# Uneven loads for uneven DMA engines: output weights and a few MLP rows split by numbers of partitions, in a single-token attention and MLP kernel

## The chip, the cores and the metric

The kernel runs on one core of a Trainium2 chip. A core has a matrix engine (TensorE, PE in the profile), a vector engine (VectorE, DVE), a scalar engine (ScalarE, ACT), GpSimd (POOL), a queue engine that issues transfers (SyncE, SP), and 16 DMA engines that move the bytes between the chip's main memory (HBM) and the core's on-chip memory. The on-chip memory has 128 partitions (rows); a tile such as `[128, 8, 512]` lies with its first index on the partitions.

The metric is the device time of one execution in microseconds. Before the change it is 194.83 us, the median of two runs (194.55 and 195.11). The profile shown is of one execution, with a span of 193.2 us.

## What is computed

One token passes a layer norm, and then two branches: attention over a cached window of 4096 positions with 32 heads, and a small MLP whose result gates it. Cut to what matters (all inputs are bf16):

```python
D, H, Dh, W, F = 512, 32, 128, 4096, 1376
xn = layernorm(x)                                    # x: [1, 1, 512]
# branch A
q = (xn @ wq)                                        # wq: [512, 4096] -> 32 heads of 128
k, v = k_cache[:, :, -W:], v_cache[:, :, -W:]        # [32 heads, 4096, 128] each
p = softmax(q @ k.T * Dh ** -0.5)                    # per head
s = (p @ v).reshape(1, 4096) @ wo                    # wo: [4096, 512]
# branch B: z = layernorm(xn); the first part's shifts leave only zeros for one token
x1 = xn + zeros @ w2
m = x1 + gelu(layernorm(x1) @ w3) @ w4               # w3: [512, 1376], w4: [1376, 512]
out = x + s * silu(m)
```

The keys and values of the window are 32 MiB each, the weights some 11 MB more. All of it is read once.

## The kernel before

The heads are worked off in eight groups of four (`G = 4`). The loop runs ten times: in step `s` the keys of group `s` are loaded and scored, and the values of group `h = s - 2` are loaded and weighted. There are three buffers for keys and two for values. A load of keys or values of one group is 4 MB, on 128 partitions of 32 KB.

All large loads go through one helper, and so through one issuing queue, in program order:

```python
def load(dst, src):
    return tc.keep_in_program_order(nc.sync.dma_start(out=dst, in_=src))
```

The start of the program (two small loads of x go through ScalarE's queue instead):

```python
nc.scalar.dma_start(out=x_bf[:], ...)                # 1 KB
nc.scalar.dma_start(out=x_row[0:P:32, :], ...)       # 1 KB, 4 partitions
load(w2_sb[:], ...)                                  # 512 KB
load(w3_sb[:], ...)                                  # 1376 KB
load(w4_sb[:, 0:10, :], ...)                         # 1280 KB
load(w4_sb[0:96, 10, :], B_w4[10 * P:F, :])          # the last 96 rows of w4, 1 KB each
load(wq_sb[:]..., A_wq.rearrange("(a b c) n -> b a (c n)", a=2, c=KC))   # 4 MB
...                                                  # then, in the loop, keys and values
```

The semaphores that report a load's completion are given out by the framework; the kernel's text names none.

The output weights `wo` have 32 row blocks of 128 rows, one for each head. They are used in four pieces:

```python
blocks = [(0, 16), (16, 8), (24, 8)]   # first head, number of heads
few_block = 2
few_h = 24
FEW = 8 * 8 * NE                       # NE = 5: 320 rows
h_part = few_h + FEW // P              # 26
r_part = FEW % P                       # 64

def load_wo(i):                        # heads 0-15, heads 16-23: n KB per partition
    h0, n = blocks[i]
    load(wo_blk[i], A_wo[h0 * P:(h0 + n) * P, :].rearrange("(p t) n -> p t n", p=P))

def load_few():                        # heads 24, 25 and half of 26: 2 x 20 partitions of 8 KB
    t = wo_blk[few_block]
    for c in range(2):
        r0 = few_h * P + c * FEW // 2
        load(t[32 * c:32 * c + 4 * NE],
             A_wo[r0:r0 + FEW // 2, :].rearrange("(b a t) n -> a b (t n)", b=4, a=NE))

def load_rows(h, n):                   # one row per partition for each head; half of head 26 first
    if h == h_part:
        load(wo_rows[r_part:P, 0, :], A_wo[h * P + r_part:(h + 1) * P, :])
        h, n = h + 1, n - 1
    load(wo_rows[:, h - h_part:h - h_part + n, :],
         A_wo[h * P:(h + n) * P, :].rearrange("(h p) n -> p h n", p=P))
```

A block that lies with several rows on one partition needs its attention output spread over the partitions in the same order: `ox_spread` (VectorE) and `ox_pick` (one matmul and two VectorE operations) do this with masks made at the start; for the 20-partition part `ox_few` adds a matmul with a selector `few` and a copy. `y_block` and `y_head` then add the products to the output row, as matmuls of 1x128.

The loop, cut to the loads and to the last two steps:

```python
for s in range(NG + LAG):              # NG = 8, LAG = 2
    h = s - LAG
    last = h == NG - 1
    kn = load_kv(k_pool, A_k_cache, s, ...) if s < NG else None
    ...
    if last:
        load_rows(h_part, 2)                               # rest of head 26, head 27
        v = load_kv(v_pool, A_v_cache, h, (0, 64, 112, CP))  # 2048, 1536 and 512 KB
        for r, n in ((H - G, 2), (H - 2, 1), (H - 1, 1)):  # heads 28-29, 30, 31
            load_rows(r, n)
    elif h >= 0:
        v = load_kv(v_pool, A_v_cache, h)
    if h == 3:
        load_wo(0)
    if h == 5:
        load_wo(1)
        load_few()
    ...
    elif s == NG:                                          # the seventh group of values
        ...; y_block(1); v_part(h, v); v_out(h)
        ox_spread(few_block); ...; ox_pick(few_block); ox_few(few_block)
    else:                                                  # the last group of values
        v_part(h, v, 0, cuts[1])
        y_block(few_block)
        for r in range(h_part, H - G):
            y_head(r)
        ...                                                # rest of the values
        v_out(h)
        for r in range(H - G, H):
            y_head(r)
# y = y_ps * g_row; out_row = y + x_row; store
```

Of the kernel before, what the change touches and what calls it, by code (L numbers as in the profile page):

```python
# [8 lines left out]
P = 128  # L9
BF16 = mybir.dt.bfloat16  # L10
FP32 = mybir.dt.float32
# [7 lines left out]
G = 4  # L19
LAG = 2  # L20
K_BUFS = 3
NE = 5
# [7 lines left out]
def kernel(  # L30
# [14 lines left out]
    nc = tc.nc  # L45

    Bb, Sq, D = A_x.shape
# [9 lines left out]
    KC = D // P  # L57
# [20 lines left out]
    def load(dst, src):  # L78
        return tc.keep_in_program_order(nc.sync.dma_start(out=dst, in_=src))
# [9 lines left out]
    load(w3_sb[:], B_w3.rearrange("(p c) n -> p c n", p=P))  # L89
    w4_sb = wts.tile([P, 11, D], BF16, name="w4_sb")  # L90
    load(w4_sb[:, 0:10, :], B_w4[0:10 * P, :].rearrange("(p c) n -> p c n", p=P))
    load(w4_sb[0:96, 10, :], B_w4[10 * P:F, :])
    wq_sb = wts.tile([P, KC, HD], BF16, name="wq_sb")

    load(wq_sb[:].rearrange("p c n -> p (c n)"), A_wq.rearrange("(a b c) n -> b a (c n)", a=2, c=KC))

    def load_kv(pool, cache, g, cuts=(0, CP)):
        t = pool.tile([P, CP, Dh], BF16, tag="kv", name="kv")
# [48 lines left out]
    def rows_add(ps, col, w, last):  # L147
        k = col.shape[0]
        for j in range(KC):
            nc.tensor.matmul(ps[32 * j:32 * j + 1, :], lhsT=col, rhs=w[0:k, j * P:(j + 1) * P],  # L150
                             start=False, stop=last, skip_group_check=True)
# [31 lines left out]
    nc.vector.tensor_copy(out=xn_bf[:], in_=xn_f[:])  # L183


    perm = wts.tile([P, P // 2, 2], BF16, name="perm")
    nc.vector.tensor_copy(out=perm[:], in_=ident_bf[:].rearrange("k (a b) -> k b a", a=2))
    xq_ps = ps_tr.tile([P, KC], FP32, tag="pt", name="xq_ps")
    nc.tensor.matmul(xq_ps[:], lhsT=perm[:].rearrange("k b a -> k (b a)"), rhs=xn_bf[:], start=True, stop=True)
    xq_bf = small.tile([P, KC], BF16, name="xq_bf")  # L190
# [67 lines left out]
        nc.scalar.copy(out=q_bc[:, i:i + 4, :], in_=qb_ps[:])  # L258
    make_masks(16)
    make_masks(8)  # L260

    few = const.tile([P, 2, 32], BF16, name="few")
    nc.vector.memset(few[:], 0.0)
    for c in range(2):
        nc.vector.tensor_copy(
            out=few[:, c, 0:4 * NE].rearrange("p (a b) -> p a b", b=4),
            in_=ident_bf[:, 4 * NE * c:4 * NE * (c + 1)].rearrange("p (b a) -> p a b", b=4))

# [107 lines left out]

    blocks = [(0, 16), (16, 8), (24, 8)]
    few_block = 2
    few_h = blocks[few_block][0]
    FEW = 8 * 8 * NE
    h_part = few_h + FEW // P

    r_part = FEW % P
    o_blk, wo_blk, ox_blk = {}, {}, {}

    def load_wo(i):
        h0, n = blocks[i]
        load(wo_blk[i], A_wo[h0 * P:(h0 + n) * P, :].rearrange("(p t) n -> p t n", p=P))

    def load_few():
        t = wo_blk[few_block]
        for c in range(2):  # L400
            r0 = few_h * P + c * FEW // 2
            load(t[32 * c:32 * c + 4 * NE],
                 A_wo[r0:r0 + FEW // 2, :].rearrange("(b a t) n -> a b (t n)", b=4, a=NE))

    def wo_row(h):
        return wo_rows[:, h - h_part, :]

    def load_rows(h, n):
        if h == h_part:
            load(wo_rows[r_part:P, 0, :], A_wo[h * P + r_part:(h + 1) * P, :])  # L410
            h, n = h + 1, n - 1
        load(wo_rows[:, h - h_part:h - h_part + n, :],
             A_wo[h * P:(h + n) * P, :].rearrange("(h p) n -> p h n", p=P))

# [25 lines left out]
    def v_out(g):  # L440
        h = G * g
        b = [i for i, (h0, _) in enumerate(blocks) if h >= h0][-1]
        if b not in o_blk:
            o_blk[b] = sm_pool.tile([P, blocks[b][1]], BF16, tag=f"o{b}", bufs=1, name="o")
            if b == few_block:
                nc.gpsimd.memset(o_blk[b][:], 0.0)
        c = h - blocks[b][0]
        if g >= NG - 2:
            nc.vector.tensor_tensor(out=o_blk[b][:, c:c + G], in0=st[g]["oT"][:], in1=st[g]["rden"][:],  # L449
                                    op=ALU.mult)  # L450
            return
        for k in range(G):
            nc.scalar.mul(o_blk[b][:, c + k:c + k + 1], st[g]["oT"][:, k:k + 1], st[g]["rden"][:, k:k + 1])  # L453


    def ox_spread(i):
        n = blocks[i][1]
        to, mt, mh = masks[n]
        spread = sm_pool.tile([P, n, n], BF16, tag=f"spread{n}", bufs=1, name="spread")
        nc.vector.tensor_tensor(out=spread[:], in0=o_blk[i][:].unsqueeze(2).to_broadcast([P, n, n]),  # L460
                                in1=mt[:].unsqueeze(1).to_broadcast([P, n, n]), op=ALU.mult)
        ox_blk[i] = spread
# [12 lines left out]
                                    op=ALU.add)  # L475
        ox_blk[i] = ox

    def ox_few(i):
        of_ps = ps_misc.tile([64, 8], FP32, tag="misc", name="of_ps")
        nc.tensor.matmul(of_ps[:], lhsT=few[:].rearrange("p a b -> p (a b)"), rhs=ox_blk[i][:],  # L480
                         start=True, stop=True)
        of = sm_pool.tile([64, 8], BF16, tag="of", bufs=1, name="of")
        nc.vector.tensor_copy(out=of[:], in_=of_ps[:])
        ox_blk[i] = of


    y_row = small.tile([1, D], FP32, name="y_row")

    yr = {}
# [9 lines left out]
            nc.scalar.copy(out=y_row[:], in_=yr[i][:])  # L499

    def y_block(i):
        for t in range(8):
            rows_add(y_ps, ox_blk[i][:, t:t + 1], wo_blk[i][:, t, :], False)

    def y_head(h):
        rows_add(y_ps, o_blk[few_block][:, h - few_h:h - few_h + 1], wo_row(h), h == H - 1)

    NG = H // G
    cuts = (0, 64, 112, CP)
# [4 lines left out]
    for s in range(NG + LAG):  # L514
        h = s - LAG
        last = h == NG - 1
        kn = load_kv(k_pool, A_k_cache, s, (0, 64, CP) if s == 0 else (0, CP)) if s < NG else None
        if s == LAG:
            wts_guard.__exit__(None, None, None)
            v_pool = ctx.enter_context(tc.tile_pool(name="v", bufs=V_BUFS))  # L520
            wo_blk[few_block] = v_pool.tile([64, 8, D], BF16, tag="wo_few", bufs=1, name="wo_few")
            nc.gpsimd.memset(wo_blk[few_block][:], 0.0)
            wo_rows = v_pool.tile([P, H - h_part, D], BF16, tag="wo_rows", bufs=1, name="wo_rows")
            nc.gpsimd.memset(wo_rows[0:r_part, 0, :], 0.0)
        if last:
            load_rows(h_part, 2)
            v = load_kv(v_pool, A_v_cache, h, cuts)
            for r, n in ((H - G, 2), (H - 2, 1), (H - 1, 1)):
                load_rows(r, n)
# [3 lines that stand above are left out]
            wo_24 = k_pool.tile([P, 32, D], BF16, tag="kv", name="wo_24")  # L533
            wo_blk[0], wo_blk[1] = wo_24[:, 0:16, :], wo_24[:, 16:24, :]
            load_wo(0)
        if h == 5:
            load_wo(1)
            load_few()

        if s < NG:  # L540
            nb = len(batches(s))

            def keys(b0, b1):
                for b in range(b0, b1):
                    k_turn(s, kn, b)
                    if b > 0:
                        k_scores(s, b - 1)

            k_open(s)
            k_vector(s, kn, 0)  # L550
            keys(0, 2)
            if s > 1:
                sm_den(s - 2)
                sm_rden(s - 2)
            if h - 1 in MOVED:
                v_add(h - 1)
                v_out(h - 1)
            keys(2, 4)
            k_vector(s, kn, 1)
            if s > 0:  # L560
                sm_turn(s - 1)
            if s == 6:
                ox_spread(0)
            keys(4, nb)
            k_scores(s, nb - 1)
            sm_own(s)
            if s > 0:
                sm_exp(s - 1)
            k_vector(s, kn, 2)
            if s == 6:  # L570
                ox_pick(0)
            k_vector(s, kn, 3)
            if h >= 0:
                v_part(h, v)
            sm_max(s)
            if s == 6:
                y_wide(0, 0, 16)
            if h >= 0 and h not in MOVED:
                v_out(h)
        elif s == NG:  # L580

            sm_den(NG - 2)
            sm_rden(NG - 2)
            sm_turn(NG - 1)
            ox_spread(1)
            sm_exp(NG - 1)
            ox_pick(1)
            y_block(1)
            rows_add(y_ps, one_f, y_row, False)
            v_part(h, v)  # L590
            v_out(h)
            ox_spread(few_block)
            sm_den(NG - 1)
            sm_rden(NG - 1)
            ox_pick(few_block)
            ox_few(few_block)
        else:
            v_part(h, v, 0, cuts[1])
            y_block(few_block)
            for r in range(h_part, H - G):  # L600
                y_head(r)
            for c0, c1 in zip(cuts[1:], cuts[2:]):
                v_part(h, v, c0, c1)
            v_out(h)
            for r in range(H - G, H):
                y_head(r)
# [36 lines left out]
```

## Time and profile before

| | |
|---|---|
| time, median of two runs | 194.83 us |
| span of the profiled execution | 193.2 us |
| read from main memory | 78.84 MB, 408 GB/s over the span |
| TensorE matmul busy | 132.6 us (69%) |
| VectorE busy | 143.8 us (74%) |
| ScalarE busy | 87.1 us (45%) |
| GpSimd busy | 6.4 us (3%) |
| shares of the chain that ended last | VectorE 50%, DMA 24%, TensorE 16% |

How to read the page. The span is cut into 40 equal slices; a digit is the busy share of an engine in a slice in tenths, 9 for 90% or more. The row named DMA is the mean busy share of the 16 DMA engines, and the row below it is what they moved. A queue's line gives its packets, its megabytes, and the time of its packets as a share of 16 engines times the span. The chain that ended last is followed back from the last instruction, at each step to what released it. In the list of waits a row names who waited, on what, for how long in total, how often, and the longest. In the timeline a row gives start, length, engine, source line, operation and names; SPq is the issuing queue, and the length of its rows is that of the issue, not of the transfer. Each load reports its completion by semaphore increments, one for each DMA engine that took part; their times are in the trace as well.

### The profile page before, as it was taken

How to read it: one execution, taken by the hardware profiler on the slowest of the kernel's cores; microseconds unless marked ns; L12 is line 12 of the kernel's file. 1: busy time of each engine (PE TensorE's matmuls, PEld its weight loads, DVE VectorE, ACT ScalarE, POOL GpSimd, SP SyncE). 2: the span in 40 equal slices, each digit the busy share in tenths (PEclk: the TensorE clock that was granted, in tenths of full speed). 3: DMA queues.
4: the chain of work that ended last, by engine and by line, in shares of the span. 5: the costliest groups of instructions: out<-in, count | busy, mean ns of one | idle time of the engine just before them, and what ended most of it. 6: DMA issues, size and time to landing. Idle time of an engine off the chain costs nothing.

```text
span 193.2 us, 4769 instructions
## 1 busy us (share of the span) xinstructions
PE 132.6 (69%) x2123; PEld 102.3 (53%) x2123; DVE 143.8 (74%) x162; ACT 87.1 (45%) x195; POOL 6.4 (3%) x14
## 2 busy tenths in 40 slices
PE   0549763977736579798898938840878879845792
PEld 0444463866625433486884428740768257733771
DVE  0560208999999999999999999990899999931201
ACT  2003002888896360468568044731574077813000
POOL 2110008000000000000000000000000000000000
PEclk9999955588755557978559995855576696755555
DMA  6999999999999999999999999999999999999980
GB/s 205 417 472 427 397 427 453 421 427 424 434 431 434 434 433 421 434 427 434 424 431 434 431 434 407 461 431 434 431 427 426 427 424 407 458 417 377 416 326 8
DMA packets 4725, 79.13 MB, mean 410 GB/s; under 512 B 666, under 2 KB 1466, under 8 KB 1722
## 3 DMA queue, kind: packets, MB, share of 16 engines
q1 hardware_dynamic: 4554, 78.84, 96.0%
q8 instruction: 16, 0.26, 0.5%
q10 hardware_dynamic: 152, 0.00, 0.0%
q14 instruction: 3, 0.02, 0.0%
HBM read 78.84 MB, written 0.00 MB: 408 GB/s over the span
## 4 chain that ended last, share of the span: by engine, by line
DVE 50%; DMA 24%; PE 16%; issue 5%; ACT 3%; POOL 1%; SPq 0%; ACTq 0%; POOLq 0%
DVE S L310 29%; DVE prod L308 16%; DMA kv<-in_A_k_cache_dram 14%; DMA kv<-in_A_v_cache_dram 8%; PE oT L430 3%; PE yr_ps L496 3%; ACT kt L326 2%; DMA x_bf<-in_A_x_dram 2%; PE qT_ps L244 2%; PE hr_ps L228 2%; PE a_ps L217 1%; PE pt L324 1%; PE hr_ps L225 1%; PE sT L332 1%; DVE S L346 1%
## 5 line engine op out<-in xcount | busy, mean ns | idle before, releaser
L310 DVE TENSOR_REDUCE S<-prod 128x20 f32<-128x2560 bf16 (+2 forms) x32 | 82.2, 2570 | 1.1
L326 ACT COPY kt<-pt 128x1024 bf16<-128x1024 bf16 (+1 forms) x56 | 54.5, 1007 | 20.9 <-PE pt L324 20.3
L324 PE MATMUL pt<-ident_bf,kv 128*128 128x128 bf16 x444 | 47.1, 276 | 7.1 <-DMA kv<-in_A_k_cache_dram 7.1
L308 DVE TENSOR_TENSOR prod<-kv,q_bc 128x2560 bf16<-128x2560 bf16 (+2 forms) x32 | 43.5, 1360 | 7.6 <-DMA kv<-in_A_k_cache_dram 4.9
L324 PEld LDWEIGHTS <-kv 128*128 128x128 bf16 x444 | 38.0, 127 | 9.2 <-DMA kv<-in_A_k_cache_dram 7.9
L332 PE MATMUL sT<-qT_bf,kt 128*128 128x4 bf16 x444 | 20.6, 168 | 16.9 <-ACT kt L326 16.3
L332 PEld LDWEIGHTS <-kt 128*128 128x128 bf16 x444 | 17.1, 103 | 24.5 <-ACT kt L326 24.1
L430 PE MATMUL oT<-pT,kv 128*128 128x4 bf16 x768 | 21.8, 166 | 7.6 <-issue 5.5
L430 PEld LDWEIGHTS <-kv 128*128 128x128 bf16 x768 | 21.1, 103 | 9.6 <-issue 5.7
L422 PE MATMUL ov<-kv,pT 128*16 128x512 bf16 x64 | 16.6, 425 | 0.0
L370 ACT ACTIVATE pT<-S,mb 128x128 bf16<-128x128 f32 x32 | 13.9, 570 | 0.3
L453 ACT ACTIVATE o<-oT,rden 128x1 bf16<-128x1 f32 x24 | 4.3, 261 | 15.5 <-PE oT L430 9.0
L422 PEld LDWEIGHTS <-pT 128*16 128x16 bf16 x64 | 6.1, 98 | 9.5 <-issue 3.5
L449 DVE TENSOR_TENSOR o<-oT,rden 128x4 bf16<-128x4 f32 x2 | 0.3, 162 | 12.4 <-PE oT L430 12.4
L341 ACT ACTIVATE own<-sT,par 128x48 f32<-128x48 f32 (+2 forms) x32 | 7.6, 361 | 3.6 <-PE sT L332 3.1
L370 ACT ACTIVATION_READ_ACCUMULATOR pT<-S,mb 128x1 f32 x32 | 8.2, 255 | 0.0
L231 DVE COPY hr<-hr_ps 1x512 f32<-1x512 f32 x1 | 0.7, 679 | 8.3 <-PE hr_ps L228 8.3
L425 ACT COPY ov_sb<-ov 16x512 f32<-16x512 f32 x2 | 1.1, 575 | 12.1 <-PE ov L422 12.1
L437 PE MATMUL oT<-ident_f,ov_sb 16*128 16x4 f32 x16 | 2.9, 301 | 4.1 <-DVE rden L381 4.1
L496 PE MATMUL yr_ps<-wo,ox 128*1 128x512 bf16 x16 | 4.9, 476 | 1.2 <-DVE ox L474 1.2
L220 ACT ACTIVATE a_bf<-a_ps 128x10 bf16<-128x10 f32 x1 | 0.2, 179 | 12.1 <-PE a_ps L217 12.1
L354 PE MATMUL mt_ps<-ident_f,m 128*1 128x128 f32 x8 | 2.8, 354 | 3.3 <-DVE rden L381 3.3
(117 smaller groups left out, 92.0 us busy)
## 6 DMA issues: line engine op xcount, KB each, us to landing
kv<-in_A_k_cache_dram SPq DMA_DIRECT2D x7, 4096.0 KB, 29.4
kv<-in_A_v_cache_dram SPq DMA_DIRECT2D x7, 4096.0 KB, 33.8
wq_sb<-in_A_wq_dram SPq DMA_DIRECT2D x1, 4096.0 KB, 18.4
kv<-in_A_k_cache_dram SPq DMA_DIRECT2D x2, 2048.0 KB, 22.6
wo<-in_A_wo_dram SPq DMA_DIRECT2D x1, 2048.0 KB
kv<-in_A_v_cache_dram SPq DMA_DIRECT2D x1, 2048.0 KB, 11.9
kv<-in_A_v_cache_dram SPq DMA_DIRECT2D x1, 1536.0 KB, 15.0
w_sb<-in_B_w_dram SPq DMA_DIRECT2D x1, 1376.0 KB
```

The lines of the kernel that those rows point to most:

```text
L228: nc.tensor.matmul(hr_ps[:], lhsT=a_bf[0:m, i:i + 1], rhs=w4_sb[0:m, i, :], start=False, stop=(i == len(chunks) - 1))
L308: nc.vector.tensor_tensor(out=prod[:, 0:m, :], in0=kn[:, rows, :], in1=q_bc[:, g:g + 1, :].to_broadcast([P, m, Dh]), op=ALU.mult)
L310: nc.vector.tensor_reduce(out=st[g]["S"][:, rows], in_=prod[:, 0:m, :], axis=AX.X, op=ALU.add)
L324: nc.tensor.transpose(pt[:, c - c0, :], kn[:, c, :], ident_bf[:])
L326: nc.scalar.copy(out=kts[b][:, 0:c1 - c0, :], in_=pt[:, 0:c1 - c0, :])
L332: nc.tensor.matmul(st[g]["sT"][:, c - nd(g), :], lhsT=kt[:, c - c0, :], rhs=qT_bf[:, G * g:G * g + G], start=True, stop=True)
L341: nc.scalar.mul(s["own"][:, 0:m, a], s["sT"][:, 0:m, a], par[:, a:a + 1])
L370: nc.scalar.activation(out=s["pT"][:, :, a], in_=s["S"][:], func=ACT.Exp, scale=scale, bias=mb[:, a:a + 1], accum_out=s["sum"][:, a:a + 1])
L422: nc.tensor.matmul(s["ov"][:], lhsT=s["pT"][:, c:c + 4, :].rearrange("p i a -> p (i a)"), rhs=v[:, c:c + 4, :], start=(c == 0), stop=(c == ...
L430: nc.tensor.matmul(s["oT"][:], lhsT=v[:, c, :], rhs=s["pT"][:, c, :], start=(c == 0), stop=(c == CP - 1))
L453: nc.scalar.mul(o_blk[b][:, c + k:c + k + 1], st[g]["oT"][:, k:k + 1], st[g]["rden"][:, k:k + 1])
L496: nc.tensor.matmul(yr[i][:], lhsT=ox_blk[i][:, t:t + 1], rhs=wo_blk[i][:, t, :], start=(t == 0), stop=(t == n - 1))
```

## The change

Loads that run on all 16 DMA engines are replaced by pairs or series of loads whose numbers of partitions differ, such as 120 and 8, [...]. It is meant to even out when the engines finish. The 20-partition loads, which gave five engines a share of their own, and what they need (`few`, `ox_few`, two memsets of tiles, half rows of head 26) are taken out. Heads 24 to 27 become a block of their own with four rows on a partition; heads 28 to 31 stay single rows. wq's rows are taken in four parts instead of two, with the permutation of x that fits.

```diff
-    load(w4_sb[0:96, 10, :], B_w4[10 * P:F, :])
+    p0 = 0
+    for n in (7, 6, 5, 4, 3, 2, 1, 64, 4):
+        load(w4_sb[p0:p0 + n, 10, :], B_w4[10 * P + p0:10 * P + p0 + n, :])
+        p0 += n
...
-    load(wq_sb[:]..., A_wq.rearrange("(a b c) n -> b a (c n)", a=2, c=KC))
+    load(wq_sb[:]..., A_wq.rearrange("(a b c) n -> b a (c n)", a=4, c=KC))
...
-    perm = wts.tile([P, P // 2, 2], BF16, name="perm")
-    nc.vector.tensor_copy(out=perm[:], in_=ident_bf[:].rearrange("k (a b) -> k b a", a=2))
+    perm = wts.tile([P, P // 4, 4], BF16, name="perm")
+    nc.vector.tensor_copy(out=perm[:], in_=ident_bf[:].rearrange("k (a b) -> k b a", a=4))
...
+    make_masks(4)
...                                            # the selector `few` goes
-    blocks = [(0, 16), (16, 8), (24, 8)]
+    blocks = [(0, 16), (16, 8), (24, 4), (H - G, G)]
+    h_part = H - G
...
-    def load_wo(i):
+    def load_wo(i, parts=((0, P),)):
         h0, n = blocks[i]
-        load(wo_blk[i], A_wo[h0 * P:(h0 + n) * P, :].rearrange("(p t) n -> p t n", p=P))
+        src = A_wo[h0 * P:(h0 + n) * P, :].rearrange("(p t) n -> p t n", p=P)
+        for (t0, p), (t1, _) in zip(parts, parts[1:] + ((n, P),)):
+            load(wo_blk[i][0:p, t0:t1, :], src[0:p, t0:t1, :])
+            if p < P:
+                load(wo_blk[i][p:P, t0:t1, :], src[p:P, t0:t1, :])
...                                            # load_few, the half rows and ox_few go
         if h == 5:
-            load_wo(1)
-            load_few()
+            load_wo(1, ((0, 120), (1, 104), (3, 88)))
+            load_wo(2, ((0, 72),))
...
         if last:
-            load_rows(h_part, 2)
...
-            ox_spread(few_block)
+            ox_spread(2)
             sm_den(NG - 1)
             sm_rden(NG - 1)
-            ox_pick(few_block)
-            ox_few(few_block)
+            ox_pick(2)
         else:
             v_part(h, v, 0, cuts[1])
-            y_block(few_block)
-            for r in range(h_part, H - G):
-                y_head(r)
+            y_block(2)
```

Heads 16 to 23 are thus loaded as row 0 of each partition in 120 and 8 partitions, rows 1 and 2 in 104 and 24, rows 3 to 7 in 88 and 40; heads 24 to 27 in 72 and 56.

More of the change, by code (lines that the diff above doesn't have):

```diff
@@ L91 @@
     load(w4_sb[:, 0:10, :], B_w4[0:10 * P, :].rearrange("(p c) n -> p c n", p=P))
-    load(w4_sb[0:96, 10, :], B_w4[10 * P:F, :])
+    p0 = 0
+    for n in (7, 6, 5, 4, 3, 2, 1, 64, 4):
+        load(w4_sb[p0:p0 + n, 10, :], B_w4[10 * P + p0:10 * P + p0 + n, :])
+        p0 += n
     wq_sb = wts.tile([P, KC, HD], BF16, name="wq_sb")
-    load(wq_sb[:].rearrange("p c n -> p (c n)"), A_wq.rearrange("(a b c) n -> b a (c n)", a=2, c=KC))
+    load(wq_sb[:].rearrange("p c n -> p (c n)"), A_wq.rearrange("(a b c) n -> b a (c n)", a=4, c=KC))
     def load_kv(pool, cache, g, cuts=(0, CP)):
@@ L260 @@
     make_masks(8)
[L264 to L269, printed above, removed]
+    make_masks(4)
     y_ps = ps_y.tile([P, P], FP32, name="y_ps")
@@ L381, in sm_rden @@
         nc.vector.reciprocal(out=s["rden"][:], in_=s["den"][:])
-    blocks = [(0, 16), (16, 8), (24, 8)]
[L386 to L391, printed above, removed]
+    blocks = [(0, 16), (16, 8), (24, 4), (H - G, G)]
+    h_part = H - G
     o_blk, wo_blk, ox_blk = {}, {}, {}
-    def load_wo(i):
+    def load_wo(i, parts=((0, P),)):
         h0, n = blocks[i]
-        load(wo_blk[i], A_wo[h0 * P:(h0 + n) * P, :].rearrange("(p t) n -> p t n", p=P))
[L398 to L403, printed above, removed]
+        src = A_wo[h0 * P:(h0 + n) * P, :].rearrange("(p t) n -> p t n", p=P)
[3 more added lines that the diff above has]
+                load(wo_blk[i][p:P, t0:t1, :], src[p:P, t0:t1, :])
     def wo_row(h):
@@ L408, in load_rows @@
     def load_rows(h, n):
-        if h == h_part:
-            load(wo_rows[r_part:P, 0, :], A_wo[h * P + r_part:(h + 1) * P, :])
-            h, n = h + 1, n - 1
         load(wo_rows[:, h - h_part:h - h_part + n, :],
@@ L444, in v_out @@
             o_blk[b] = sm_pool.tile([P, blocks[b][1]], BF16, tag=f"o{b}", bufs=1, name="o")
-            if b == few_block:
-                nc.gpsimd.memset(o_blk[b][:], 0.0)
         c = h - blocks[b][0]
@@ L476, in ox_pick @@
         ox_blk[i] = ox
[L478 to L484, printed above, removed]
     y_row = small.tile([1, D], FP32, name="y_row")
@@ L501, in y_block @@
     def y_block(i):
-        for t in range(8):
+        for t in range(blocks[i][1]):
             rows_add(y_ps, ox_blk[i][:, t:t + 1], wo_blk[i][:, t, :], False)
     def y_head(h):
-        rows_add(y_ps, o_blk[few_block][:, h - few_h:h - few_h + 1], wo_row(h), h == H - 1)
+        rows_add(y_ps, o_blk[3][:, h - h_part:h - h_part + 1], wo_row(h), h == H - 1)
     NG = H // G
@@ L520 @@
             v_pool = ctx.enter_context(tc.tile_pool(name="v", bufs=V_BUFS))
-            wo_blk[few_block] = v_pool.tile([64, 8, D], BF16, tag="wo_few", bufs=1, name="wo_few")
-            nc.gpsimd.memset(wo_blk[few_block][:], 0.0)
+            wo_blk[2] = v_pool.tile([P, 4, D], BF16, tag="wo_4", bufs=1, name="wo_4")
             wo_rows = v_pool.tile([P, H - h_part, D], BF16, tag="wo_rows", bufs=1, name="wo_rows")
-            nc.gpsimd.memset(wo_rows[0:r_part, 0, :], 0.0)
         if last:
-            load_rows(h_part, 2)
             v = load_kv(v_pool, A_v_cache, h, cuts)
```

## The prediction

> **What bounds the kernel now.** I read the slices of the span first, then the queues, then the busy time by stretches, and only then the chain of waits. The page of the kernel before:
>
> ```profile
> DVE  0560208999999999999999999990899999931201
> DMA  6999999999999999999999999999999999999980
> GB/s 205 417 472 427 397 427 453 421 427 424 434 431 434 434 433 421 434 427 434 424 431 434 431 434 407 461 431 434 431 427 426 427 424 407 458 417 377 416 326 8
> ...
> q1 hardware_dynamic: 4554, 78.84, 96.0%
> ```
>
> The second line is the busy share of the 16 DMA engines: 9 or more in every slice between the first and the last two. The one queue that carries all the loads fills 96.0% of 16 engines times the span. VectorE is nearly as full in the middle, but it is idle in the last eighth. The stretches say the same (columns: stretch, length, busy time of the engines, clock, DMA share, GB/s):
>
> ```profile
> 12.00:60.00 48.00, 33.60 (x509) 26.46 (x509) 31.89 (x32) 25.39 (x43) 4.49 (x3) 0.72 1.00 429
> 60.00:110.00 50.00, 40.71 (x482) 27.93 (x481) 49.32 (x37) 27.10 (x66) 0.00 (x0) 0.72 1.00 430
> 110.00:160.00 50.00, 33.08 (x548) 26.61 (x547) 44.19 (x37) 23.55 (x56) 0.00 (x0) 0.69 1.01 431
> 160.00:187.00 27.00, 19.51 (x486) 16.41 (x485) 12.52 (x21) 9.75 (x31) 0.00 (x0) 0.56 0.98 406
> ```
>
> DMA share 1.00 from 12 to 160 us: no hole in which a delay could be caught up. The chain of waits ends in the same resource, a load of V of 14.97 us and 3.2 us of work after it:
>
> ```profile
> 171.96 14.97 DMA kv<-in_A_v_cache_dram
> 186.93 0.05 issue
> 186.98 1.88 PE oT L430 x64
> 188.86 0.02 issue
> 188.88 0.17 DVE o L449
> 189.06 0.04 issue
> 189.10 0.69 PE y_ps L150 x16
> ```
>
> So the end is: first packet at 1.74 us, bytes at full rate, skew between the 16 engines, then about 3.7 us from the last landing (189.44) to the end of the span. A lost microsecond of all engines is a microsecond of the total. A better balance can win only the skew: the 16 completions of the last load run from 185.56 to 189.44 us and have a mean of 188.0, so perfect balance is worth 1.4 us.
>
> The third view is what the issuing queue waits for, and the one the change turns on:
>
> ```profile
> SPq L79 <- DMA w_sb<-in_B_w_dram: 4.1, 2, 3.8
> ...
> SPq L79 <- DMA x_row<-in_A_x_dram: 0.9, 1, 0.9
> SPq L79 <- DMA x_bf<-in_A_x_dram: 0.8, 1, 0.8
> ```
>
> The loads of K that wait there need neither x tile; the 3.8 us run from the end of the third K issue, 7.48, to the last completion of w4's main part, 11.27. In the trace all DMAs of the program use eight completion semaphores in strict rotation, and a DMA is not issued until the eighth DMA before it has landed completely:
>
> ```profile
> 2.75 0.66 SPq L79 DMA_DIRECT2D wq_sb<-in_A_wq_dram  x1
> 4.85 0.54 SPq L79 DMA_DIRECT2D kv<-in_A_k_cache_dram  x1
> 6.94 0.54 SPq L79 DMA_DIRECT2D kv<-in_A_k_cache_dram  x1
> 177.93 0.33 SPq L79 DMA_DIRECT2D wo_rows<-in_A_wo_dram  x1
> ```
>
> x_bf landed at 4.83 and K's second half was issued at 4.85; x_row landed at 6.92 and the third K load was issued at 6.94; V of the seventh group landed at 177.91 and the last row load was issued at 177.93. Three times 0.02 us.
>
> [...] each of the two 20-partition loads shows 11 increments at once and five later ones, and their issue took 0.92 and 0.76 us against 0.54 to 0.60. [...] here the first packet began 1.02 us after the start of the first issue (0.72), whose instruction took 0.39, so 0.63 after its end. [...] a 1 KB packet takes 0.046 us and an 8 KB one 0.309, so eight small ones cost 0.06 us more.
>
> **The change, part by part.** *Bytes by engine.* [...] The completions of the heads 16 to 23 load come in groups: four at 163.8, two at 164.2, six at 165.1 to 165.5, four at 167.1. The five that go on with the 20-partition loads are three of the early and two of the middle ones. [...] The lateness grows with the 16 KB packets of the instruction queue (about 1.06 us each, on one engine at a time); four more of them come after 165 us.
>
> *Issues.* w4's rows: one DMA becomes nine. Heads 16 to 27: five loads (one block, two of 20 partitions, two of rows) become eight. [...]
>
> *The rotation at the start.* Number the DMAs in program order: x_bf 0, w2 1, x_row 2, w3 3, w4's main part 4, its nine small loads 5 to 13, wq 14. Number 11 waits for w3 (7.90), and number 12, the 64-row load, for w4's main part, whose last completion is at 11.27. By then the queue holds nothing but small rows and runs dry: the last main packets end between 10.2 and 10.7. From 11.29: 0.6 for number 12, 0.85 for number 13, then wq is issued at about 12.8, first packet 1.0 later at about 13.8. Before, wq's first packets began at 10.40 to 10.97, mean 10.73. **Loss: 3.1 us on all engines.** The query projection starts at 23.01 and wq was landed at 21.15, so the compute side slips by only 21.15 + 3.1 − 23.01 = 1.2 us and gates nothing more than before.
>
> *The rotation at heads 16 to 27.* Numbers 31 to 38 wait for numbers 23 to 30, the last for the V load of the sixth group, which lands at 164.74 (all times of this part plus 3.1). Only after it comes the seventh V load, which before was issued at 149.26 and lay ready. Now: 164.76 + 0.8 + 1.0 gives a first packet at about 166.6. An early engine has finished its 129 KB (5.0 us) by 165.7 and waits; a middle one starts V at about 167.4; [...] From 166.6: V 9.7, the last V 9.84 (8 packets each of 0.611, 0.460 and 0.159), 32 KB of rows at 0.046 make 1.5, landing 0.55: 188.2; plus 0.8 for the middle engines or 1.1 for one that meets an instruction packet: 189.0 to 190. Before it was 189.44. **Gain of the balance: between +0.4 and −0.5, say 0.2.**
>
> *The rest.* The matmuls, selector and memsets of the 20-partition part go: 24 of 1x128 matmuls fewer in the last stage, but they lie between two landings of V and cost nothing now. The order of wq's rows in four parts instead of two, with the matching permutation, moves the same 32 KB packets. Both 0.
>
> *Sum:* 194.83 + 3.1 − 0.2 = 197.7; I take 197.5, since the start may restart a little sooner.
>
> **Rivals.** (1) Balance wins: the waits of the rotation fall into time when the queue is still full, [...] up to 1.4 us of skew goes: 193.6. [...] Against: 3 MB of weights are all that is queued before number 12, and they are gone by 10.7. (2) Balance is wrong: [...] with the loss at the start 194.83 + 3.1 + 1.5 = 199.4. Against: nothing in the groups of completions speaks for it, and the wait at 164.7 evens the engines out anyway. (3) Only issue costs count, with no rotation: 15 or so issues beside a full queue are hidden, 194.8. Against: the three 0.02 us.
>
> **Range and chances.** The loss at the start rests on three measured waits; its size is uncertain by 0.5. The tail is uncertain by 1 each way. Eight in ten: 195.3 to 199.0. Slower by over 2% starts at 198.73: 0.17. Faster by over 2% ends at 190.9, which even perfect balance would not reach: 0.02. Within 2%: 0.81.
>
> **What would show it.** In the profile after: a DMA share clearly under 1 between 11 and 14 us; the issuing queue waiting for w4's load before wq is issued near 12.8; wq's landing near 24.2; the seventh V load issued near 169 instead of 149 with a wait on V before it; the last completions within 3 us of each other. It is wrong if wq is issued by 8 us, or if the queue is dry nowhere and the span is shorter.

## The result and the profile after

The changed kernel takes 206.91 us (206.78 and 207.03), against 194.83 before: 1.061 times as long, with a 95% interval of 1.058 to 1.064. The prediction was 197.5 with a range of 195.3 to 199.0. The same bytes are loaded, and the engines compute as much as before (VectorE 144.0 us, ScalarE 87.0, TensorE 133.7). The time went into the transfers, in two places. The page of the changed kernel, the slices and the queue that carries the loads:

```profile
DVE  1550108997999999999999999927999999020101
DMA  6949999999999999999999999999999999999970
GB/s 203 424 127 409 422 435 467 404 435 451 435 412 409 454 433 428 422 435 438 432 422 412 428 419 470 419 425 428 441 420 422 425 275 189 242 435 387 416 279 9
...
q1 hardware_dynamic: 4775, 78.84, 93.9%
```

A slice is now 5.1 us. The third, from 10.3 to 15.4 us, shows the first place: DMA share 4 and 127 GB/s. The second place is in slices 33 to 35, from 164 to 179 us: the DMA row still says 9, but the bytes fall to 275, 189 and 242 GB/s. The row of shares alone would not have shown it. A DMA engine counts as busy while one of its packets is under way, however slowly (0.92 at 183 GB/s, below).

The same two places, cut by stretches (stretch, length, busy time of the engines, clock, DMA share, GB/s). A packet counts whole in the stretch in which it begins, so a share can pass 1. First the change's:

```profile
8.00:10.50 2.50, 0.76 (x4) 0.61 (x3) 1.96 (x14) 0.00 (x0) 0.18 (x1) 1.00 0.94 398
10.50:12.00 1.50, 0.59 (x2) 0.54 (x3) 1.30 (x10) 0.00 (x0) 0.09 (x1) 1.00 0.04 12
12.00:14.00 2.00, 1.22 (x22) 1.22 (x22) 1.30 (x8) 0.00 (x0) 0.47 (x1) 1.00 0.68 182
14.00:16.00 2.00, 1.68 (x27) 1.62 (x26) 0.00 (x0) 0.40 (x3) 0.00 (x0) 1.00 0.83 311
...
163.00:168.00 5.00, 4.13 (x86) 3.42 (x84) 4.92 (x6) 4.55 (x6) 0.00 (x0) 1.00 0.89 291
168.00:173.00 5.00, 2.71 (x80) 2.35 (x76) 4.91 (x3) 4.07 (x15) 0.00 (x0) 0.92 0.92 183
173.00:178.00 5.00, 1.90 (x72) 1.84 (x69) 1.50 (x3) 0.00 (x0) 0.00 (x0) 0.50 1.14 235
```

Then the kernel before at the same stages:

```profile
10.50:12.00 1.50, 0.59 (x2) 0.54 (x3) 1.30 (x11) 0.00 (x0) 0.03 (x1) 1.00 1.22 498
...
165.00:170.00 5.00, 4.03 (x134) 3.90 (x134) 4.90 (x5) 3.15 (x14) 0.00 (x0) 0.67 1.08 460
```

Between 10.5 and 12 us the queue is as good as empty (0.04, 12 GB/s) where it was full. Between 168 and 173 us it is full and slow (0.92, 183 GB/s). What holds the start is in the chain of waits of the changed kernel, in order of time:

```profile
1.64 9.57 DMA w_sb<-in_B_w_dram
11.20 0.02 issue
11.22 0.66 SPq L79
11.88 0.04 issue
11.93 0.46 SPq L79
12.39 0.04 issue
12.43 0.62 SPq L79
```

The 64-row load is issued 0.02 us after the last landing of w4's main part (11.20), then the 4-row load, then wq at 12.43. The change moves wq's issue from 2.75 to 12.43 us, and wq's last landing from 21.15 to 25.04.

In the tail the packets themselves are slower. Their durations are in the trace. Mean of the packets that start between 166 and 168 us:

```
packet            before    change    at the rate of 8 KB in 0.309 us
 2 KB               -        0.142       0.077
 5 KB               -        0.340       0.193
32 KB             1.213      1.899       1.236
```

From 173 to 177 us the 32 KB packets, which are those of the seventh V load, take 2.2 to 2.9 us. So not only the uneven loads are slow. What is under way beside them is slow as well, large packets too.

The seventh V load itself, issued at 149.26 us before, now waits until the sixth has landed (171.48) and then the 120-partition load (171.88):

```profile
171.94 0.54 SPq L79 DMA_DIRECT2D kv<-in_A_v_cache_dram  x1
```

### The profile page after: what moved, and what is told of

Read it like the earlier page. It is cut to its first block, busy times and chain, and to the rows that moved or that the text cites. A ratio compares the mean times of both kernels' runs of the same rounds, so it can differ in the third digit from the quotient of the medians.

```text
span 205.0 us, 4728 instructions
## 1 busy us (share of the span) xinstructions
PE 133.7 (65%) x2098; PEld 101.2 (49%) x2098; DVE 144.0 (70%) x162; ACT 87.0 (42%) x195; POOL 2.4 (1%) x11
## 4 chain that ended last, share of the span: by engine, by line
DMA 44%; DVE 21%; PE 19%; ACT 7%; issue 4%; SPq 3%; ACTq 0%
DMA kv<-in_A_v_cache_dram 19%; DVE S L303 13%; DMA kv<-in_A_k_cache_dram 11%; DMA wo_rows<-in_A_wo_dram 10%; DVE prod L301 6%; ACT kt L319 6%; PE oT L412 5%; PE ov L404 5%; DMA w_sb<-in_B_w_dram 5%; PE pt L317 5%; SPq L79 3%; PE sT L325 2%; PE mb_ps L356 1%; PE den_ps L369 1%; PE oT L419 1%
## 5 line engine op out<-in xcount | busy, mean ns | idle before, releaser
L317 PE MATMUL pt<-ident_bf,kv 128*128 128x128 bf16 x444 | 45.8, 271 | 12.3 <-DMA kv<-in_A_k_cache_dram 12.3
L317 PEld LDWEIGHTS <-kv 128*128 128x128 bf16 x444 | 37.2, 124 | 14.3 <-DMA kv<-in_A_k_cache_dram 12.7
L412 PEld LDWEIGHTS <-kv 128*128 128x128 bf16 x768 | 21.3, 104 | 18.0 <-DMA kv<-in_A_v_cache_dram 10.8
L404 PE MATMUL ov<-kv,pT 128*16 128x512 bf16 x64 | 18.8, 466 | 0.0
L404 PEld LDWEIGHTS <-pT 128*16 128x16 bf16 x64 | 6.6, 105 | 11.2 <-issue 6.5
L467 PE MATMUL yr_ps<-wo,ox 128*1 128x512 bf16 x16 | 5.6, 529 | 0.9 <-DVE ox L454 0.9
L247 PE MATMUL qT_ps<-xq_bf,wq_sb 128*128 128x1 bf16 x128 | 3.5, 165 | 3.2 <-DMA wq_sb<-in_A_wq_dram 3.2
L356 PE MATMUL mb_ps<-md,par_t 5*128 5x4 f32 x16 | 4.2, 329 | 1.7 <-DVE md L351 1.0
```

Of the source, the lines that this page charges most:

```text
L317: nc.tensor.transpose(pt[:, c - c0, :], kn[:, c, :], ident_bf[:])
L356: nc.tensor.matmul(mb_ps[:], lhsT=par_t[:].rearrange("k b a -> k (b a)"), rhs=md[:], start=True, stop=True)
L404: nc.tensor.matmul(s["ov"][:], lhsT=s["pT"][:, c:c + 4, :].rearrange("p i a -> p (i a)"), rhs=v[:, c:c + 4, :], start=(c == 0), stop=(c == ...
L412: nc.tensor.matmul(s["oT"][:], lhsT=v[:, c, :], rhs=s["pT"][:, c, :], start=(c == 0), stop=(c == CP - 1))
L467: nc.tensor.matmul(yr[i][:], lhsT=ox_blk[i][:, t:t + 1], rhs=wo_blk[i][:, t, :], start=(t == 0), stop=(t == n - 1))
```

## The experiments

Two theories come out of this. **Rotation:** the start is lost because nine DMAs instead of one push wq round the ring of eight completion semaphores, behind w4's main part. **Partitions:** the tail is lost because of the partitions that a load of other than 128 partitions writes: transfers that write certain partitions at the same time slow one another (the "collisions" of the expectations). Why they should do so was a supposition of the author's about the on-chip side; no trace shows it, nor how the rows of a load are dealt to the engines. The rivals: unequal bytes, small or strided packets, the held-back V load, the number of DMAs, the pieces of HBM.

All ratios below are to the kernel before, run on the same chips.

**The start alone.**

```diff
 # kernel before
-    load(w4_sb[0:96, 10, :], ...)
+    for n in (7, 6, 5, 4, 3, 2, 1, 64, 4): load(...)      # as in the change
```

> The kernel before with w4's last 96 rows in the nine uneven loads and nothing else. Theory of the semaphore rotation: the 64-row load waits for the landing of w4's main part, wq is issued near 12.4 us instead of 2.75 and lands near 24.9 instead of 21.15, and every later landing keeps the delay: +4.0 us, 198.8. Rival, issue cost only: nine issues beside a full queue are hidden, 194.8. Rival, the start is only a part of a delay that grows by itself: over 201.

Measured: 199.23 us, 1.019 (1.014 to 1.024). The DMA share from 10.5 to 12 us, as a stretch of this run:

```profile
10.50:12.00 1.50, 0.59 (x2) 0.55 (x3) 1.30 (x9) 0.00 (x0) 0.25 (x1) 1.00 0.01 3
```

wq was issued at 12.07. The start costs 1.9% by itself, about 3.7 us, and nothing grows out of it later.

**The tail alone.**

```diff
 # changed kernel
-    for n in (7, 6, 5, 4, 3, 2, 1, 64, 4): load(...)
+    load(w4_sb[0:96, 10, :], ...)
```

> The changed kernel with w4's last rows in one load, as before. Rotation at the start and another cause in the tail, which add up: 206.9 - 4.0 = 202.9, with the slow 32 KB packets (2 us and more instead of 1.21) still there while the uneven output weights land. Rival, the tail's loss comes from the late start (the engines are out of step because of it): below 197.

Measured: 203.06 us, 1.038 (1.033 to 1.043). The stretch of the slow packets:

```profile
165.00:170.00 5.00, 3.11 (x88) 2.93 (x89) 4.93 (x3) 3.62 (x14) 0.00 (x0) 0.57 0.82 152
```

152 GB/s with a start that is in step: the tail's loss doesn't come from the late start. 1.9% and 3.8% make 5.7% of the 6.1%, within the intervals.

**The nine loads behind wq.**

```diff
 # changed kernel
-    for n in (7, 6, 5, 4, 3, 2, 1, 64, 4): load(...)      # before wq
     load(wq_sb[:]...)
+    for n in (7, 6, 5, 4, 3, 2, 1, 64, 4): load(...)      # after wq
```

> The changed kernel with the nine small loads kept, but issued after wq instead of before it. Rotation: wq is in the queue at about 2.8 us, the queue does not run dry, the waits are hidden behind wq's 9.6 us: the same as with one load, 202.9 within 0.6. Rival, the nine loads cost by being small and on few engines, wherever they stand: 206 to 207.

Measured: 207.13 us, 1.058 (1.052 to 1.064): nothing came back, and by the numbers of the expectation the rival won. But the expectation had counted wrongly. With wq as DMA number 5, the 64-row load is number 13 and waits for wq itself. The issuing queue's waits in this run:

```profile
SPq L79 <- DMA wq_sb<-in_A_wq_dram: 9.5, 1, 9.5
```

The 64-row load was issued at 20.80, the first load of K at 21.96, and slices 4 and 5 move 351 and 167 GB/s. The hole has moved ten microseconds down; it has not closed. This run could not separate the two.

**Six loads instead of nine.**

```diff
 # kernel before
-    load(w4_sb[0:96, 10, :], ...)
+    for n in (7, 6, 5, 4, 64, 10): load(...)
```

> The kernel before with w4's last 96 rows in six uneven loads (7, 6, 5, 4, 64, 10 rows) instead of nine. Rotation: wq is now DMA number 11 and waits for w3, which lands near 7.9, not for w4's main part; it is issued near 8.5, while the queue is still full, and the 4 us of the nine loads are gone altogether: 195 to 196. Rival, uneven small loads cost as such: two thirds of the loss stays, about 198.4.

Measured: 195.50 us, 1.001 (0.999 to 1.004). wq was issued at 7.80, and the queue stays full:

```profile
10.50:12.00 1.50, 0.51 (x2) 0.46 (x3) 1.30 (x9) 0.00 (x0) 0.36 (x1) 1.00 1.47 546
```

Six uneven loads cost nothing and nine cost 3.7 us. That is a matter of which earlier DMA the ring puts ahead of wq's issue (w3, landed at 7.8, or w4's main part, landed near 11), not of small or uneven loads. The start is settled.

**No balance at all.**

```diff
 # tail alone
-            load_wo(1, ((0, 120), (1, 104), (3, 88)))
-            load_wo(2, ((0, 72),))
+            load_wo(1)
+            load_wo(2)
```

> The changed kernel with w4's rows in one load and heads 16 to 23 and 24 to 27 in one 128-partition load each: no balance at all, neither the five-engine share nor the uneven loads. If the uneven loads themselves cost the tail's 8 us, this gives them all back but loses the five-engine share of before (the late engines carry 102 KB instead of 82, 0.8 us): 195.6. Rival, the four-row block of heads 24 to 27 or wq in four parts costs something: over 198.

Measured: 195.39 us, 0.999 (0.997 to 1.001). This is the base line for the next runs, and it clears the new block of heads 24 to 27 and wq in four parts of any cost. It also says that the five-engine share of the kernel before wins nothing that these runs can measure.

**The same eight loads, on all partitions.**

```diff
 # no balance at all
-            load_wo(1)
-            load_wo(2)
+            six loads of heads 16-23, all 128 partitions, rows 0,1,2,3,4-5,6-7 of each
+            two loads of heads 24-27, all 128 partitions, rows 0-1, 2-3
```

> As the run with no balance at all, but heads 16 to 27 in eight loads of 128 partitions each (six and two, cut along the rows of a partition), so the same number of DMAs as in the change, and the seventh V load is held back until the sixth has landed. If holding V back is the cause: the early engines idle about 2 us, the late ones are the bound, and if that spreads, 198 to 203. If the partition ranges of the uneven loads are the cause: the packets keep their usual 1.21 us per 32 KB, the late engines never run dry, 195.4 to 196.4.

Measured: 197.00 us, 1.009 (1.006 to 1.011). The last of the eight loads was issued at 165.33 and the seventh V load at 165.75, held back too, though 2.8 us less than in the tail alone (168.52). The stretch:

```profile
165.00:170.00 5.00, 4.19 (x125) 3.89 (x123) 4.90 (x4) 4.21 (x15) 0.00 (x0) 0.68 0.97 342
```

The 2 KB packets, which skip through HBM in the same strides as the change's, take 0.092 us in the mean (0.151 in the tail-alone run). The first packets of V after the hold take 1.5 to 2.2 us on most engines and 1.21 from then on, as after the empty queue at the start (about 2.0 us there on most engines, then 1.23). Strides, small packets, the number of DMAs and a hold of this length together make 1.0%. It is a little more than the theory of the partitions had allowed (196.4); which of them costs it was not tested apart.

**The seventh V load not held back.**

```diff
 # tail alone
             load_wo(1, ((0, 120), (1, 104), (3, 88)))
-            load_wo(2, ((0, 72),))
+        if h == 6:                                        # behind the seventh V load
+            load_wo(2, ((0, 72),))
```

> The changed kernel with w4's rows in one load, and the two loads of heads 24 to 27 issued after the seventh V load instead of before it, so that this V load is not held back to the landing of the sixth. If the uneven partition ranges are the main cause, the slow packets stay and the middle engines need about 10 us instead of 5 for their share of heads 16 to 23: 199 to 201. If the held-back V load is the main cause: 195 to 197.

Measured: 206.06 us, 1.052 (1.047 to 1.057), more than both expectations. V was issued at 155.21, before the sixth had landed. But the two uneven loads of heads 24 to 27 now land beside the last V load, and its 16 KB packets take 0.9 to 1.5 us from 181 to 188 us, against 0.611 before. The slow stretch has moved to a later place; why it costs more there was not tested.

**Heads 16 to 23 uneven, nothing else.**

```diff
 # seventh V load not held back
         if h == 6:
-            load_wo(2, ((0, 72),))
+            load_wo(2)
```

> The changed kernel with w4's rows in one load, heads 16 to 23 uneven as in the change, heads 24 to 27 in one load of 128 partitions behind the seventh V load, which is not held back. Only the uneven 1 MB is left of the change's tail. If collisions while it lands are the cause, a good part stays: 200 to 202. If the held-back V load or heads 24 to 27 carry the loss: under 197.

Measured: 201.30 us, 1.031 (1.029 to 1.034). One megabyte in uneven loads, with no V load held back, costs 3.2% over no balance at all:

```profile
165.00:170.00 5.00, 3.38 (x96) 3.08 (x94) 4.93 (x3) 3.96 (x15) 0.00 (x0) 0.63 1.15 246
```

**Equal bytes, half the partitions.**

```diff
 # no balance at all
-            load_wo(1)
+            load_wo(1, ((0, 64),))                        # 64 and 64 partitions
```

> As the run with no balance at all, but heads 16 to 23 in two loads of 64 partitions each. Every engine gets the same bytes as from one load of 128, the number of loads rises by one, nothing waits. [...] the 8 KB packets take up to twice 0.309 us [...], and 32 KB packets beside them suffer too: 197 to 199. If only unequal bytes or small packets hurt: 0.309 and 195.4.

Measured: 201.01 us, 1.027 (1.022 to 1.032). Every engine carries the same bytes in the same 8 KB packets as with one load, if all 16 take part, as they do in the 64-row load of w4 in the changed kernel (16 landings, 13.18 to 13.42 us); three loads, nothing waits. The stretches, the first of no balance at all and the other three of this run:

```profile
165.00:170.00 5.00, 4.43 (x140) 4.32 (x141) 4.93 (x3) 3.60 (x14) 0.00 (x0) 0.58 1.08 457
...
160.00:165.00 5.00, 3.79 (x75) 2.96 (x73) 4.90 (x6) 4.79 (x6) 0.00 (x0) 1.00 1.05 279
165.00:170.00 5.00, 2.58 (x82) 2.48 (x83) 4.93 (x4) 3.15 (x14) 0.00 (x0) 0.83 0.92 197
170.00:175.00 5.00, 2.58 (x65) 2.13 (x62) 0.76 (x3) 0.72 (x4) 0.00 (x0) 0.50 1.04 341
```

The 8 KB packets take 0.592 us in the mean instead of 0.309. The 32 KB packets of V beside them take 2.0 to 2.4 us, and the 4 KB packets of heads 24 to 27 take 0.286 in the mean. All three are near twice the usual (0.309, 1.21 and 0.159). The loss was larger than expected (197 to 199). Unequal bytes are not needed for it.

**The same halves, on every second partition.**

```diff
 # equal bytes, half the partitions
-            rows 0-511 to partitions 0-63,           rows 512-1023 to partitions 64-127
+            rows 0-511 to partitions 0, 2, ..., 126, rows 512-1023 to partitions 1, 3, ..., 127
```

> As the run with two loads of 64 partitions: the same two pieces of HBM, the same 8 KB packets, the same bytes on each engine, but the first load goes to the even partitions and the second to the odd ones, [...]. (The rows of heads 16 to 23 thus land at other partitions than the output spread expects; the output is not the reference's, the work is the same.) [...] most of the loss goes: packets well under 0.59 us, 195.4 to 197.5. If the two pieces of HBM or the number of 64 rows is the cause: 0.59 and 201.

Measured: 195.51 us, 1.001 (0.999 to 1.003); the whole loss is gone.

```profile
160.00:165.00 5.00, 3.88 (x75) 3.03 (x73) 4.90 (x6) 4.78 (x6) 0.00 (x0) 1.00 0.94 398
165.00:170.00 5.00, 4.24 (x142) 4.03 (x142) 4.93 (x3) 3.58 (x14) 0.00 (x0) 0.89 1.11 470
170.00:175.00 5.00, 1.83 (x10) 1.29 (x10) 1.99 (x9) 1.43 (x8) 0.00 (x0) 0.50 0.96 410
```

197 GB/s become 470 in the same stretch, and 0.592 us a packet become 0.313. The pieces of HBM, the 64 rows and the 8 KB packets are the same in both; only the partitions differ. For these two loads this run decides between the on-chip side and HBM.

**A share for eight engines.**

```diff
 # kernel before
-NE = 5                                # heads 24, 25, half of 26 on 2 x 20 partitions
+NE = 8                                # heads 24 to 27 on 2 x 32 partitions, meant as 4 for each engine
-            load_rows(h_part, 2)      # and the half rows of head 26
```

> The kernel before with a share for eight engines instead of five: heads 24 to 27 in two loads of 32 partitions, split over eight engines with four partitions each, and no half rows. [...] there are three DMAs fewer. If collisions and waits are all that was wrong with the change: 8 KB packets at 0.309 us and 193.8 to 195.2. If any share for few engines costs: over 196.

Measured: 195.50 us, 1.002 (1.000 to 1.004). All 192 packets of 8 KB take 0.309 us. An uneven share of this form does no harm here. And it wins nothing either: 14 engines have their last load by 188.16 us, two at 189.9, against 189.44 for the last one before. No version here is measurably faster than the kernel before.

## Why the prediction was wrong

**The loss at the start: right in mechanism, 0.8 us short.** The three waits of 0.02 us had been read rightly. The first wq packet came at 13.84 us where "about 13.8" was predicted, but by luck, since two errors cancelled. The 4-row load's issue took 0.46 us, not 0.85, so wq was issued at 12.43, not 12.8; and from there to the first packet it was 1.41 us, not 1.0. (The change's uneven loads on fewer than 16 engines took 0.22 to 0.59 us to issue; the 0.85 was that of the 20-partition loads.) The term that was too small is the restart of an empty queue. wq's first packets began at a mean of 14.06 us instead of 10.68 (the prediction read 10.73), and the first packet of most engines took about 2.0 us instead of 1.3. Together this put wq's last landing 3.9 us later, not 3.1, and the first K landings as well (29.54 instead of 25.60). The loss in time is 3.7 us by the run of the start alone.

**The work of the tail: the step that failed.** A rate of 0.0386 us per KB, from the 8 KB packets of the kernel before (0.309/8), stands behind the prediction's 5.0 us for 129 KB on an engine that takes part in all eight loads, and was used for all uneven loads: an early engine was to finish its share by 165.7 plus the start's delay. In the change, the early engines landed V's sixth load from 165.60 and their last part of heads 16 to 23 from 171.79. That is 6.2 us for 89 KB, the share of an engine that takes part in all six loads, where the rate gives 3.4. The 20-partition loads of the kernel before have the rate, as have the 8 KB packets of its 128-partition load (all 168 packets take 0.309 to 0.318 us); two loads of 64 neighbouring partitions do not (0.592). The prediction asked how many bytes each engine gets and never which partitions the loads write. That the uneven loads are slow for the same reason as the halves is the likely reading, but it is argued and not shown.

**The held-back V load: right in mechanism, with a landing that was off.** It was issued at 171.94 us, not near 168.7, because the landing ahead of it was itself late: the four late engines landed the sixth V load at 170.79 to 171.48, while the twelve others were done by 168.31. Its first packet began at 173.57, where the prediction's path gives 169.7 (166.6 and 3.1 for the start). Its packets then took some 12.5 us on the engine that finished first, where 9.7 was reckoned. The rest of that engine's way took 11.7 us, much as reckoned (11.9). These two terms make the 6.6 us by which the first engine ended later (197.92) than the prediction's path (188.2 and 3.1). Where the packets of V are back at 1.21 us after the first, as with the eight even loads, the hold and all that goes with it cost 1.0%.

**The gain of the balance, "0.2": none was seen, and its aim was off.** Which engines a load on fewer than 16 uses was the author's assumption; the trace names no engine. What it shows is how many: each of the uneven loads has one semaphore update near its issue and then one for each engine that lands its part, 15 for 120 partitions, 8 for 8, 13 for 104, 12 for 24, 11 for 88 and 10 for 40 (5 for the 20 partitions of the kernel before; the prediction's "11 increments at once" are one early update there, whose amount the trace does not give). The sixth V load lands in groups of six early, six middle and four late engines; the 15-engine load in 5, 6 and 4, so the engine that it leaves out is an early one. The 13-engine load has two late ones, the 12-engine load one, the 11-engine load none. So the late engines were relieved, but each of these four loads has five early ones of the six; if the missing one is the same engine each time, it was given the greatest relief, for nothing. The tail alone gives the same counts; in the two runs that released V the groups run together.

**The rivals.** "Balance is wrong", 199.4, had the right sign for a different reason: not the wrong engines but, by the likely reading, the wrong partitions. "Only issue costs" and "balance wins" fell with the start alone and the tail alone. Of what the prediction had named as signs, wq's issue near 12.8 (12.43), the hole between 11 and 14 us and the late V load came true; wq's landing near 24.2 (25.04) and the last completions within 3 us of each other (197.92 to 201.41) did not.

**What stays open.** How the held-back V load and the slow packets share the tail's 3.8% can't be read off, since each run that released V also moved other loads. Why two loads of 64 neighbouring partitions are slow was not seen: the trace names neither a packet's engine nor the rows that an engine moves. That the uneven loads lose for the same reason rests on the halves and on what the even loads rule out: no run sent the same uneven rows to other partitions. What is shown is that the two loads of 64 rows lose or keep their full rate with their destination partitions alone (0.592 us for 8 KB against 0.313).

## What to carry to other kernels

Count a load's cost by the partitions it writes, not only by its bytes. Of the splits of a large load tried here, two kept the full rate: every second partition (8 KB in 0.313 us), and the shares of 20 and of 32 partitions (0.309). Halves of 64 neighbouring partitions (0.592) and the uneven parts (2 KB in 0.142, where that rate gives 0.077) lost it, and slowed the transfers beside them. Before adding small loads to a saturated queue, number all DMAs and see which landing each one waits for; six were free, and nine cost 3.7 us. And look at GB/s beside the busy share of the DMA engines: the share read 0.92 and 1.14 while 183 and 235 GB/s moved, where 431 is the usual rate.

## What was not expected of the hardware

The slowness reaches beyond the loads that bring it: 32 KB packets of an ordinary load rose from 1.21 to as much as 2.9 us. Two loads of 64 neighbouring partitions, 1 MB in all, cost 5.5 us over one load of 128. An empty queue is slow to restart: the first 32 KB packet on most engines took about 2.0 us, against 1.3 behind other packets. And four DMA engines are late at the sixth V load (170.79 to 171.48 us, the other twelve by 168.31), while the one that the 120-partition load leaves out is, by the counts above, among the early ones.
